# Batch 0 of an attention and two-MoE kernel: which engine masks its high parts and copies its second heads, on which line its value loads stand, and what the planner books for a conversion

## The chip, the cores and the metric

The kernel runs on one core of a Trainium2 chip. The metric is the device time of one execution in microseconds (us). Engines are PE (TensorE; its weight loads are PEld), DVE (VectorE), ACT (ScalarE), POOL (GpSimd) and SP (SyncE, which here only issues DMAs). Each engine works off its own queue in order and stands still at an instruction whose semaphore has not come.

## The reference

Three layers in a row, all in float32:

```python
# attention: B, H, S, D = 4, 8, 576, 64; rotate() is rotary position embedding
scores = (rotate(q) @ rotate(k).T) / sqrt(D)
attn   = softmax(scores)                      # max, exp, sum
x      = (attn @ v) -> [2304, 512]
# MoE 1: 512 -> 2048 -> 512, leaky relu with a slope alpha per column
h = x @ w_in;  g = max(h, 0) + alpha * min(h, 0);  x = g @ w_out
# soft MoE 2: 8 experts x 4 slots
logits = x @ phi;  d = softmax over tokens;  c = softmax over slots
slot_in = d.T @ x;  slot_out[e] = relu(slot_in[e] @ w1[e]) @ w2[e];  out = c @ slot_out
```

## The kernel before

**How the work is tiled.** Attention runs over 4 batches (b) of 4 pairs of heads (p). For a pair, `prep_qk` loads keys and queries with their half-swapped copies (tile `xn`, 128 partitions x 2 x 576), multiplies by the rotary tables and adds (lines 320 and 323; on DVE for the very first pair, on POOL for all others), and splits the sum into a high part (`hi`, line 326, which writes `xn[:, 1]`) and a low rest (`lo`, line 329, on DVE). DMAs on SP's queue stack the two parts into the tiles `ks` (line 346) and `qs` (line 343), so that one matmul sums both. `row_events` then makes the five row blocks of a pair (four of 128 rows for each of two heads, and a tail): scores on PE (line 385) into PSUM, a maximum on DVE (line 390), exp on ACT (line 395), a reciprocal on DVE (lines 402 and 403), the scaling on POOL (line 427), and then a transposition of the probabilities into the tile `ET`. Batches 1 to 3 transpose through DVE blocks and a round trip through DRAM. Batch 0 (`MOVED = 1`) transposes on PE (line 448) and copies PSUM to `ET` (`turned`, line 457). `pv_events` multiplies by the values (line 527) and writes `xt`, the input of MoE 1.

**Weights.** Meanwhile `prep_w` makes 16 pieces ready, eight of `w_in` and eight of `w_out`: a load of 1 MB (`wraw`, line 578, three buffers), three DVE instructions that convert 64-bit floats to 32-bit ones (lines 598, 600 and 602), and for `w_in` a bound on ACT (610), a scaling on POOL (613), and a rest on PE (267, 268). Odd pieces of `w_in` sit for a time in buffers of `xt` (`wx`), so the first `pv` of a full block waits for the last of them. Pieces of `w_out` are written to DRAM (`wo_dram`, line 623) from a single buffer (`wf`), and multiplied with `phi` (lines 647 to 659).

**MoE 1** runs over nine blocks of 256 tokens (line 684) as soon as all four pairs of a half batch are done, between the attention of later batches. The second MoE's weights are loaded at the end.

**What sets the order.** `Plan.order` simulates all operations at build time: each has an engine, a cost in ns and a due time, and a free engine takes the ready operation with the lowest due time. The order in which the operations start in the plan is the order in which each engine's instructions, and SP's DMAs, are issued on the chip. So a changed cost or a changed engine changes no duration on the chip by itself, but can change every queue's order from there on. DMAs are booked on one engine of the plan. `order_ops` keeps lines of operations that must stay in order: "load" for the loads of keys and queries, "v" for those of values.

Of the kernel before, what the change touches and what calls it, by code (L numbers as in the profile page):

```python
# [12 lines left out]
F32R = mybir.dt.float32r  # L13
I32 = mybir.dt.int32
AF = mybir.ActivationFunctionType
ALU = mybir.AluOpType
# [33 lines left out]
class Plan:  # L50
# [9 lines left out]
    def op(self, eng, cost, due, fn, deps=(), takes=(), uses=()):  # L60
        o = Op(eng, cost, due, fn, deps, takes, uses)
        for d in o.deps:
            d.after.append(o)
        for s in uses:
            s.left += 1
        self.ops.append(o)
        return o
# [95 lines left out]
def attn_moe_softmoe(ctx, tc, qx, kx, vx, w_in, w_out, alpha, phi, w1, w2, tab, msks, out):  # L163
    nc = tc.nc
# [47 lines left out]
    op = plan.op  # L212
# [67 lines left out]
    def prep_v(b, due):  # L280

        mv = vb[:, b]
        iv = viv[b] = mv[:, 8:10]
        bound = []
        for p in range(NP):
            e, sl = {}, Slot("vt")

            def load(p=p, e=e):
                e["t"] = att.tile([128, 9, D], F32, tag="vt", name="vt", bufs=5)
                nc.sync.dma_start(e["t"], vx[b, p])  # L290

            def bnd(p=p, e=e):
                junk = moe["p"].tile([128, 288], F32, tag="rl", name="junk", bufs=2)
                nc.scalar.activation(junk[:].bitcast(F16).rearrange("p (r d) -> p r d", d=D), e["t"], AF.Abs, accum_out=mv[:, 4 + p:5 + p])

            o = order_ops["v"] = op(DMA, 900, due - PRE + 2 * p, load, [order_ops["v"]], takes=[sl], uses=[sl])
            vt[b, p] = (e, sl, o)
            sj = Slot("rl")
            bound.append(op(ACT, 870, due, bnd, [o], takes=[sj], uses=[sl, sj]))
        top = op(DVE, 150, due, lambda: nc.vector.tensor_reduce(mv[:, 0:1], mv[:, 4:8], axis=AX.X, op=ALU.max), bound)  # L300
        red = top_all(due, mv[:, 0:1], mv[:, 1:2], top)
        viv_op[b] = chain(due, pow2_ops(mv[:, 2:3], mv[:, 1:2], iv[:, 0:1], iv[:, 1:2]), red)

    def prep_qk(b, p, due):

        r = {}
        s_st = {"q": Slot("Q"), "k": Slot("K")}
        ends = []
        first = b == 0 and p == 0
        eng, on, cost = (nc.vector, DVE, 650) if first else (nc.gpsimd, POOL, 1570)  # L310
        for i, (src, z) in enumerate(((kx, "k"), (qx, "q"))):
            sx, e = Slot("xn"), {}
            d = due - PRE + 3 * i if not first else -29 + 2 * i

            def load(src=src, e=e):
                e["x"] = att.tile([128, 2, S], F32, tag="xn", name="xn", bufs=3)
                nc.sync.dma_start(e["x"], src[b, p])

            def mul(w, z=z, e=e):
                eng.tensor_tensor(e["x"][:, w], e["x"][:, w], tabs[:, (0 if z == "q" else 2) + w], ALU.mult)  # L320

            def add(e=e):
                eng.tensor_tensor(e["x"][:, 0], e["x"][:, 0], e["x"][:, 1], ALU.add)  # L323

            def hi(e=e):
                nc.scalar.activation(e["x"][:, 1].bitcast(F32R), e["x"][:, 0], AF.Copy)

            def lo(e=e):
                nc.vector.tensor_tensor(e["x"][:, 0], e["x"][:, 0], e["x"][:, 1], ALU.subtract)

            def stack(w, z=z, e=e):
                if w is None:
                    if z == "q":

                        r[z] = att.tile([128, 2 * SP], F32, tag="Q", name="qs", bufs=2)
                        nc.vector.memset(r[z][:, S:S + 128], 0.0)
                    else:
                        r[z] = att.tile([128, 2, 2, S], F32, tag="K", name="ks", bufs=2)
                    return
                t, x = r[z], e["x"]  # L340
                for h in range(2):
                    if z == "q":
                        (nc.scalar if first else nc.sync).dma_start(t[64 * w:64 * w + 64, (S + 128) * h:(S + 128) * h + S], x[64 * h:64 * h + 64, 1 - w])
                    else:
                        for half in range(2):
                            nc.sync.dma_start(t[64 * half:64 * half + 64, w, h], x[64 * h:64 * h + 64, 1 - w])  # L346

            o = order_ops["load"] = op(DMA, 1700, d, load, [order_ops["load"]], takes=[sx], uses=[sx])
            o = op(on, cost, d, lambda mul=mul: mul(0), [o, tabs_op[z]], uses=[sx])
            o = op(on, cost, d, lambda mul=mul: mul(1), [o], uses=[sx, s_tabs])  # L350
            o = op(on, cost, d, add, [o], uses=[sx])
            o = op(ACT, 640, d + LEADS[0], hi, [o], uses=[sx])
            x = op(DVE, 970, d + LEADS[0], lo, [o], uses=[sx])
            n = 900 if z == "q" else 1800
            prev = order_ops.get(z)
            y = op(*((DVE, 120) if z == "q" else (None, 0)), d - 100, lambda stack=stack: stack(None), [prev], takes=[s_st[z]], uses=[s_st[z]])
            o = op(DMA, n, d - 100, lambda stack=stack: stack(0), [o, prev, y], uses=[sx, s_st[z]])
            o = op(DMA, n, d - 100, lambda stack=stack: stack(1), [x, o], uses=[sx, s_st[z]])
            order_ops[z] = o
            ends.append(o)  # L360
        qk[b, p] = (r, ends, [s_st["q"], s_st["k"]])

    def row_events(b, p, s, n, pair):
# [46 lines left out]
        evs = []  # L410
# [12 lines left out]
        for h in heads:  # L423
            def norm(h=h):
                if tail:
                    nc.gpsimd.tensor_scalar(c["e"][:, 1, 0:64], c["e"][:, 0, 512:S], c["mm"][:, 6:7], 1.0, ALU.mult, ALU.mult)
                nc.gpsimd.tensor_scalar(c["e"][:, h], c["e"][:, h], c["mm"][:, 6 + h:7 + h], 1.0, ALU.mult, ALU.mult)  # L427

            o2 = op(POOL, 1200 if tail else 820, n + h + LEADS[1], norm, [o], uses=[s_mm, s_e])
            norms.append(o2)  # L430
            if moved:
                def block(h=h):
                    if h == 0:
                        c["tb"] = att.tile([128, 16, 2, 32], F32, tag="tb", name="tb", bufs=2)
                    nc.vector.transpose(  # L435
                        out=c["tb"][:, :, h].rearrange("p (q m) j -> p q m j", q=4),
                        in_=c["e"][:, h, 64 * h:64 * h + 512].rearrange("p (m q j) -> p q m j", m=4, q=4))

                blocks.append(op(DVE, 760, n + h + LEADS[2], block, [o2] + blocks[-1:], takes=[] if h else [s_tb], uses=[s_e, s_tb]))
                continue  # L440
            s_pm = Slot("pm")

            def turn(h=h):
                if h == 0 and first:
                    open_ET()
                c["pt", h] = ps_m.tile([128, 4, 128], F32, tag="pm", name="pt")
                for i in range(4):
                    nc.tensor.transpose(c["pt", h][:, i], c["e"][:, h, 64 * h + 128 * i:64 * h + 128 * i + 128], idf)  # L448

            def turned(h=h):  # L450
                if tail:
                    dst, src = pair["ett"][:, 0:4], c["pt", h]
                else:
                    dst = pair["ET"][:, 0:2048].rearrange("p (s q m h j) -> p s h m q j", s=2, q=4, m=4, h=2)[:, s % 2, h]
                    src = c["pt", h][:].rearrange("p m (q j) -> p m q j", q=4)
                if h == 0 or b == 0:
                    nc.scalar.activation(dst, src, AF.Copy)
                else:
                    nc.vector.tensor_copy(dst, src)

            new = h == 0 and first
            o2 = op(PE, 430, n + h + LEADS[2] - ATT, turn, [o2, pair.get("turn")], takes=[s_pm, s_ET] if new else [s_pm], uses=[s_pm, s_e, s_ET])
            pair.setdefault("turn", o2)
            evs.append(op(*((DVE, 690) if h and b else (ACT, 600)), n + h + LEADS[2], turned, [o2] + evs[:1], uses=[s_pm, s_ET]))
        if moved:
            if s % 2 == 0:
                pair["s_sc"] = Slot("sc")
# [98 lines left out]
    def prep_w(j, which, due):  # L566
# [48 lines left out]
        even = w_ops.get((which, j - 1)) if j % 2 else None  # L615
        u = [s_raw, s_wx, s_w]
        o = run["raw"] = op(DMA, 2913, due + WD, load, [run["raw"]], takes=[s_raw], uses=[s_raw])
        o = op(DVE, 1000, due, lambda: conv(0), [o, even if which == 0 else None], takes=[s_wx], uses=u)
        o = op(DVE, 1400, due, lambda: conv(1), [o], uses=u)
        o = op(DVE, 1600, due, lambda: conv(2), [o], uses=u)  # L620
        if which:
            w_ops[1, j] = o
            wo_saved.append(op(DMA, 1500, due, lambda: nc.sync.dma_start(wo_dram[:, 2 * j:2 * j + 2, :], c["wo"]), [o], uses=[s_w]))
# [705 lines left out]
```

## Time and profile before

| | us |
|---|---|
| median of 3 runs | 732.61 (729.93 to 734.29) |
| profiled execution, its own time | 733.35 |
| its span, first to last instruction | 731.6 |
| PE busy | 619.4 (85% of the span) |
| DVE busy | 426.1 (58%) |
| ACT busy | 341.9 (47%) |
| POOL busy | 280.6 (38%) |

The span leaves 1.75 us of the execution's own time outside. Busy shares are averages over stages: up to about 210 us batch 0's attention and the weight pieces run together, from there to about 550 us attention and MoE 1 share PE, then MoE 1 is alone, and the last 60 us load and use the experts' weights.

### The profile page before, as it was taken

The page shows a single profiled execution, that of the slowest core. Times are in us where ns is not written, and L with a number is a line of the kernel's source. Part 1 is how long each engine was busy: PE and PEld are TensorE (multiplying, and loading weights), DVE is VectorE, ACT ScalarE, POOL GpSimd, SP SyncE. Part 2 cuts the span into 40 slices and gives each one's busy share as a digit, 9 for nine tenths or more (in the row PEclk, how much of TensorE's full clock was granted, in tenths as well). Part 3 has the DMA queues.
Part 4 walks back from the last instruction along what each step waited for, and adds up shares of the span by engine and source line. Part 5 has one row for each costly group of instructions (what it writes and reads, how often), then busy time and mean ns, then how long its engine had stood idle before and what let it go on. Part 6 is the DMA issues. An engine that isn't in the chain of part 4 may idle for free.

```text
span 731.6 us, 13978 instructions
## 1 busy us (share of the span) xinstructions
PE 619.4 (85%) x5168; PEld 460.3 (63%) x5168; DVE 426.1 (58%) x933; ACT 341.9 (47%) x840; POOL 280.6 (38%) x283
## 2 busy tenths in 40 slices
PE   0747479694999989989898999998999999997973
PEld 0543246584877767776676777786687787773442
DVE  5675854565677675769556777785662333334422
ACT  2444425573565555555554555565453343330111
POOL 0496972646253564538444574452221000000000
PEclk9958579897899999999999999999999999999998
DMA  9977646566368897998969997978744961146998
GB/s 299 327 218 203 193 153 207 164 175 229 98 225 216 256 240 227 302 267 220 270 203 292 269 275 221 237 207 245 201 118 116 407 254 59 53 164 260 409 397 300
DMA packets 82146, 167.84 MB, mean 229 GB/s; under 512 B 10656, under 2 KB 39840, under 8 KB 82080
## 3 DMA queue, kind: packets, MB, share of 16 engines
q1 hardware_dynamic: 81760, 166.37, 74.4%
q8 instruction: 41, 0.67, 0.4%
q10 hardware_dynamic: 320, 0.59, 0.4%
q14 instruction: 25, 0.20, 0.1%
HBM read 104.54 MB, written 34.08 MB: 189 GB/s over the span
## 4 chain that ended last, share of the span: by engine, by line
PE 53%; DMA 24%; DVE 6%; SPq 5%; POOL 5%; issue 3%; ACT 3%; ACTq 0%; POOLq 0%; DVEq 0%
PE ph L684 19%; PE pv L527 10%; DMA xw<-in_moe_w_dram 6%; DMA ET<-sc 6%; PE st L385 5%; PE pt L703 3%; DMA ks<-xn 3%; DMA qs<-xn 3%; DMA xn<-in_k_dram 2%; PE lg L714 2%; PE pu L808 2%; SPq L346 2%; POOL e L427 2%; PE pt L448 2%; PE wphp L656 2%
## 5 line engine op out<-in xcount | busy, mean ns | idle before, releaser
L684 PEld LDWEIGHTS <-w 128*128 128x128 f16 x1728 | 164.5, 98 | 32.1 <-issue 11.1
L684 PE MATMUL ph<-xt,w 128*128 128x256 f16 x1536 | 183.5, 273 | 0.0
L427 POOL TENSOR_SCALAR e<-e,mm 128x576 f32<-128x576 f32 x144 | 119.6, 841 | 142.4 <-DVE mm L403 86.2
L390 DVE TENSOR_REDUCE mm<-st 128x1 f32<-128x576 f32 x144 | 105.7, 743 | 36.7 <-PE st L385 31.4
L385 PE MATMUL st<-ks,qs 128*128 128x288 f32 x512 | 102.6, 330 | 26.6 <-DMA ks<-xn 19.3
L395 ACT ACTIVATE e<-st,mm 128x576 f32<-128x576 f32 x144 | 106.3, 739 | 35.4 <-DVE mm L390 31.8
L697 DVE SCALAR_TENSOR_TENSOR g<-rl,oma,ph 128x256 f32<-128x256 f32 x144 | 68.2, 474 | 77.4 <-ACT rl L692 76.5
L320 POOL TENSOR_TENSOR xn<-xn,tabs 128x576 f32<-128x576 f32 x60 | 89.4, 1503 | 62.0 <-DMA xn<-in_k_dram 29.6
L692 ACT ACTIVATE rl<-ph 128x256 f32<-128x256 f32 x144 | 55.0, 382 | 102.7 <-PE ph L684 101.8
L385 PEld LDWEIGHTS st<-ks,qs 128*128 128x128 f32 x512 | 77.9, 203 | 35.5 <-DMA ks<-xn 19.2
L527 PE MATMUL pv<-ET,vt 128*64 128x256 f32 x512 | 66.1, 402 | 18.0 <-DMA ET<-sc 14.5
L435 DVE STREAM_TRANSPOSE tb<-e 128x512 f32<-128x512 f32 x96 | 66.5, 698 | 20.5 <-DMA sc<-tb 13.2
L527 PEld LDWEIGHTS pv<-ET,vt 128*64 128x64 f32 x512 | 38.3, 141 | 38.5 <-issue 14.0
L708 ACT ACTIVATE gt<-pt 128x512 f32<-128x512 f32 x72 | 43.0, 597 | 18.1 <-PE pt L703 16.4
L448 PE MATMUL pt<-idf,e 128*128 128x128 f32 x192 | 33.3, 308 | 14.3 <-POOL e L427 14.3
L537 ACT ACTIVATE xt<-pv,vb 128x256 f16<-128x256 f32 x32 | 15.1, 473 | 64.8 <-PE pv L527 64.7
L703 PE MATMUL pt<-idf,g 128*128 128x128 f32 x288 | 43.7, 274 | 0.4 <-DVE g L697 0.4
L323 POOL TENSOR_TENSOR xn<-xn 128x576 f32<-128x576 f32 x30 | 43.5, 1453 | 0.7
L448 PEld LDWEIGHTS pt<-idf,e 128*128 128x128 f32 x192 | 25.3, 160 | 21.3 <-POOL e L427 16.5
L703 PEld LDWEIGHTS pt<-idf,g 128*128 128x128 f32 x288 | 33.7, 141 | 2.5 <-issue 0.8
L402 DVE TENSOR_SCALAR mm<-mm 128x2 f32<-128x2 f32 (+1 forms) x80 | 24.7, 309 | 15.7 <-ACT e L395 15.7
L540 DVE SCALAR_TENSOR_TENSOR xt<-pv,vb,xt 128x256 f16<-128x256 f32 x32 | 15.4, 480 | 26.3 <-ACT xt L537 26.0
(151 smaller groups left out, 819.9 us busy)
## 6 DMA issues: line engine op xcount, KB each, us to landing
sc<-tb SPq DMA_DIRECT2D x48, 512.0 KB, 6.1
ET<-sc SPq DMA_DIRECT2D x96, 256.0 KB, 5.6
xw<-in_moe_w_dram SPq DMA_DIRECT2D x42, 512.0 KB, 10.2
ks<-xn SPq DMA_DIRECT2D x128, 144.0 KB, 3.6
xn<-in_k_dram SPq DMA_DIRECT2D x16, 576.0 KB, 6.1
xn<-in_q_dram SPq DMA_DIRECT2D x16, 576.0 KB, 5.9
qs<-xn SPq DMA_DIRECT2D x60, 144.0 KB, 4.8
wraw<-in_moe_w_in_dram SPq DMA_DIRECT2D x8, 1024.0 KB, 8.3
```

The source lines that it names most:

```text
L320: eng.tensor_tensor(e["x"][:, w], e["x"][:, w], tabs[:, (0 if z == "q" else 2) + w], ALU.mult)
L385: nc.tensor.matmul(st[:, j, 0:288], r["q"][:, 768 * h + 128 * s:768 * h + 128 * s + 128].bitcast(F32R), r["k"][:, a, h, ks].bitcast(F32R), ...
L390: nc.vector.tensor_reduce(c["mm"][:, h:h + 1], c["st", h][:, :, 0:288], axis=AX.XY, op=ALU.max, negate=True)
L395: nc.scalar.activation(c["e"][:, h].rearrange("p (a n) -> p a n", a=2), c["st", h][:, :, 0:288], AF.Exp, bias=c["mm"][:, h:h + 1], accum_o ...
L427: nc.gpsimd.tensor_scalar(c["e"][:, h], c["e"][:, h], c["mm"][:, 6 + h:7 + h], 1.0, ALU.mult, ALU.mult)
L435: nc.vector.transpose(out=c["tb"][:, :, h].rearrange("p (q m) j -> p q m j", q=4), in_=c["e"][:, h, 64 * h:64 * h + 512].rearrange("p (m q ...
L448: nc.tensor.transpose(c["pt", h][:, i], c["e"][:, h, 64 * h + 128 * i:64 * h + 128 * i + 128], idf)
L527: nc.tensor.matmul(pv[r], v[k, 4 * h + i if i < 4 else 8], x, start=(i == 0), stop=(i == 4))
L684: nc.tensor.matmul(ph, wi[j][:, wp, kc, 128 * fo:128 * fo + 128], xt[:, xp, kc, :], start=(n == 0), stop=(n == 3 * KC - 1),)
L692: nc.scalar.activation(c["r"], c["ph"], AF.Relu, scale=-1.0)
L697: nc.vector.scalar_tensor_tensor(blk["g", j][:, fo, :], c["r"], oma[:, f:f + 1], c["ph"], ALU.mult, ALU.add)
L703: nc.tensor.transpose(c["pt"][:, t, i, :], blk["g", j][:, fo - 1 + i, 128 * t:128 * t + 128], idf)
```

## The change

Batch 0 only: the high part is made by DVE as a bit mask (the low 12 bits cleared) in place of ACT's rounding copy, and the copies of the second head (`h = 1`) from PSUM to `ET` go from ACT to DVE. The four value loads of batch 0 stand on the same line as the loads of keys and queries. The planner books 870, 1420 and 1250 ns for the three conversion steps, where it booked 1000, 1400 and 1600.

```diff
-            o = order_ops["v"] = op(DMA, 900, due - PRE + 2 * p, load, [order_ops["v"]], takes=[sl], uses=[sl])
+            z = "v" if b else "load"
+            o = order_ops[z] = op(DMA, 900, due - PRE + 2 * p, load, [order_ops[z]], takes=[sl], uses=[sl])
...
             def hi(e=e):
-                nc.scalar.activation(e["x"][:, 1].bitcast(F32R), e["x"][:, 0], AF.Copy)
+                if b:
+                    nc.scalar.activation(e["x"][:, 1].bitcast(F32R), e["x"][:, 0], AF.Copy)
+                else:
+                    nc.vector.tensor_scalar(e["x"][:, 1].bitcast(I32), e["x"][:, 0].bitcast(I32), -4096, None, ALU.bitwise_and)
...
-            o = op(ACT, 640, d + LEADS[0], hi, [o], uses=[sx])
+            o = op(*((ACT, 640) if b else (DVE, 870)), d + LEADS[0], hi, [o], uses=[sx])
...
-                if h == 0 or b == 0:
+                if h == 0:
                     nc.scalar.activation(dst, src, AF.Copy)
                 else:
                     nc.vector.tensor_copy(dst, src)
...
-            evs.append(op(*((DVE, 690) if h and b else (ACT, 600)), n + h + LEADS[2], turned, [o2] + evs[:1], uses=[s_pm, s_ET]))
+            evs.append(op(*((DVE, 690) if h else (ACT, 600)), n + h + LEADS[2], turned, [o2] + evs[:1], uses=[s_pm, s_ET]))
...
-        o = op(DVE, 1000, due, lambda: conv(0), [o, even if which == 0 else None], takes=[s_wx], uses=u)
-        o = op(DVE, 1400, due, lambda: conv(1), [o], uses=u)
-        o = op(DVE, 1600, due, lambda: conv(2), [o], uses=u)
+        o = op(DVE, 870, due, lambda: conv(0), [o, even if which == 0 else None], takes=[s_wx], uses=u)
+        o = op(DVE, 1420, due, lambda: conv(1), [o], uses=u)
+        o = op(DVE, 1250, due, lambda: conv(2), [o], uses=u)
```

## Rows read from the trace of the kernel before

**Rows 1.** Busy us (instructions) by stretch, then PE clock, DMA share, GB/s.

```profile
0.00:210.00 210.00, 141.26 (x860) 104.49 (x862) 130.60 (x241) 100.49 (x225) 113.46 (x105) 0.84 0.68 209
210.00:732.00 522.00, 478.17 (x4316) 355.85 (x4312) 295.53 (x692) 241.44 (x616) 167.13 (x179) 0.98 0.78 238
...
60.00:113.00 53.00, 32.57 (x123) 18.48 (x122) 36.02 (x54) 20.43 (x43) 38.26 (x32) 0.74 0.60 184
113.00:140.00 27.00, 26.14 (x209) 18.56 (x208) 10.99 (x27) 18.05 (x44) 8.68 (x11) 1.00 0.69 209
```

**Rows 2.** Chain that ended last, 0 to 210 us: first and last DVE, ACT, POOL pieces.

```profile
6.16 1.44 DVE xn L320 x2
...
8.41 0.69 ACT xn L326
...
31.29 0.61 POOL xn L320
...
190.63 0.60 ACT wt L651
...
202.14 0.17 DVE wph L659
...
208.65 0.21 POOL xn L320
```

**Rows 3.** Groups of instructions with their shapes, 0 to 210 us: busy us, mean ns.

```profile
L602 DVE SCALAR_TENSOR_TENSOR w<-wraw,w 128x1024 int32<-128x1024 int32 x12 | 18.8, 1567 | 0.0
...
L457 ACT ACTIVATE ET<-pt 128x512 f32<-128x512 f32 x32 | 18.3, 597 | 17.2 <-PE pt L448 16.7
...
L600 DVE SCALAR_TENSOR_TENSOR w<-wraw,w 128x1024 int32<-128x1024 int32 x12 | 17.1, 1429 | 0.1
...
L598 DVE TENSOR_SCALAR w<-wraw 128x1024 int32<-128x1024 int32 x12 | 9.1, 760 | 16.6 <-DMA wraw<-in_moe_w_in_dram 7.6 <-DMA wo_dram<-w 6.4 <-PE pt L448 2.1
...
L326 ACT ACTIVATE xn<-xn 128x576 fp32r<-128x576 f32 x13 | 8.8, 685 | 5.4 <-POOL xn L323 3.7 <-DVE xn L323 1.8
...
L402 DVE TENSOR_SCALAR mm<-mm 128x2 f32<-128x2 f32 x17 | 8.2, 479 | 7.9 <-ACT e L395 7.9
...
L600 DVE SCALAR_TENSOR_TENSOR wx<-wraw,wx 128x1024 int32<-128x1024 int32 x4 | 6.9, 1718 | 0.0
...
L602 DVE SCALAR_TENSOR_TENSOR wx<-wraw,wx 128x1024 int32<-128x1024 int32 x4 | 4.9, 1226 | 0.0
...
L598 DVE TENSOR_SCALAR wx<-wraw 128x1024 int32<-128x1024 int32 x4 | 2.7, 682 | 0.0
```

**Rows 4.** Single lines over the whole span: duration ns min/median/max.

```profile
L1220 DVE COPY ob<-pf x10: 680/691/693, 701.0 to 724.4; 128x512 f32<-128x512 f32 x10
...
L402 DVE TENSOR_SCALAR mm<-mm x80: 105/159/1381, 25.9 to 545.3; 128x2 f32<-128x2 f32 x64, 128x1 f32<-128x1 f32 x16
```

**Rows 5.** DVE, POOL and ACT in order of time between 74 and 88 us.

```profile
75.70 2.02 DVE L600 SCALAR_TENSOR_TENSOR wx<-wraw,wx 128x1024 int32<-128x1024 int32 x1
...
80.65 1.16 DVE L402 TENSOR_SCALAR mm<-mm 128x2 f32<-128x2 f32 x1 [0.31 <-ACT e L395]
...
80.38 2.76 POOL L320 TENSOR_TENSOR xn<-xn,tabs 128x576 f32<-128x576 f32 x2
...
74.22 0.68 ACT L326 ACTIVATE xn<-xn 128x576 fp32r<-128x576 f32 x1
...
87.61 0.68 ACT L326 ACTIVATE xn<-xn 128x576 fp32r<-128x576 f32 x1
```

**Rows 6.** SP's DMA issues in order of time, start us and issue time.

```profile
9.12 7.31 SPq L346 DMA_DIRECT2D ks<-xn  x8
...
18.30 3.04 SPq L290 DMA_DIRECT2D vt<-in_v_dram  x1
...
22.41 0.50 SPq L317 DMA_DIRECT2D xn<-in_k_dram  x1
```

**Rows 7.** DVE in order of time: the longest wait for a store.

```profile
171.57 0.75 DVE L598 TENSOR_SCALAR w<-wraw 128x1024 int32<-128x1024 int32 x1 [6.44 <-DMA wo_dram<-w]
```

## The prediction

> **What bounds the kernel now.** I read the table of stretches first. Before 210 us PE is busy for 141.3 of 210 us; after it for 478.2 of 522 [rows 1]. So PE has 68.7 us of holes early and only 43.8 late, and what the change can win or lose lies before 210 us, where all instructions it moves run. A us by which batch 0's attention ends earlier or later is carried to the end: MoE 1, which fills PE later, waits for all four pairs of a half batch, and the experts' weights wait for MoE 1's buffers. I count it one for one.
>
> Before 210 us no engine is full. DVE is busy for 130.6 us, POOL for 113.5, ACT for 100.5 [rows 1]. Of the two engines between which the change moves work, the receiver is the fuller one. The same order holds from 60 to 113 us, where the weight pieces are converted: DVE 36.0, ACT 20.4 of 53 us. It is turned round from 113 to 140 us, where ACT has 18.1 and DVE 11.0 of 27 us [rows 1].
>
> Next, the chain of what ended last. Between 0 and 210 us, of the 195 longest pieces, 32 are DVE's (22.0 us), 17 ACT's (10.2) and 18 POOL's (29.1); first and last of each are in [rows 2]. The reader is to see that one chain changes engine every us or two, so that no single operation sets this stretch. I therefore price moved work by a weight: an engine's time on the chain over its busy time. DVE 22.0/130.6 = 0.17, ACT 10.2/100.5 = 0.10, POOL 29.1/113.5 = 0.26. It says how often a us of such work has lain on the path; it is a choice, and the weakest part of the sum.
>
> **The high parts.** Four pairs with keys and queries make eight instructions. ACT loses 8 x 0.685 = 5.5 us [rows 3]. On DVE a mask of 128x576 does not occur before. Nearest is the first conversion step, also one source, a constant and 32-bit integers in SBUF: 128x1024 in 0.682 us where little disturbs it (the `wx` form, four times) [rows 3], by elements 0.38 us for 576. That is the lower bound. Above it comes time lost to POOL: the small line 402 takes 0.105 at best and 1.381 at worst [rows 4], an excess of up to 1.28 us, and the row at 80.65 us shows one that took 1.16 us while POOL's line 320 ran [rows 5]. So 0.38 to 1.66 us each. I take 0.38 plus the mean excess of line 402 before 210 us, 0.479 - 0.159 = 0.32 [rows 3, 4], that is 0.70: 5.6 us for eight, between 3.0 and 13.3.
>
> The handover also moves. Before, ACT's high part of the first keys starts at 8.41 us [rows 2] and the first stack is issued at 9.12 [rows 6]. POOL has no rotary work yet there, so the mask should take about 0.38 in place of 0.68: the first stack, and with it the first scores, come 0.3 us earlier. For the other six, DVE's mask stands in the queue that holds conversions of 1.2 to 2.4 us; the rest (`lo`) is DVE's anyway and follows directly.
>
> POOL pays in turn: six masks that meet its work hold it up by 0.38 us each at most, 2.3 us.
>
> **The copies.** Four pairs of four row blocks give 16 copies of a second head. ACT loses 16 x 0.597 = 9.6 us [rows 3]. DVE's copy of 128x512 from PSUM takes 0.691 at the median, 0.680 to 0.693 over ten [rows 4], so 16 x 0.69 = 11.0 us, with hardly a spread. The write into `ET` is strided and that row's is not; I take nothing for this, and 0.7 us each as the upper bound, a second pass of the same length (+11 us on DVE, at its weight 1.9).
>
> **The value loads.** No move: in the plan the batch's loads are due at -9 to -3, after the first queries' load (-27) and before the next keys' (0), so the joint line demands the order that SP already shows, values at 18.30 us and keys at 22.41 [rows 6]. Batch 1's first load only loses a predecessor that was long done. SP, ACT's bounds and the DMA engines see the same. If the order did change, the price is that of one blocked issue, 3.0 us [rows 6].
>
> **The planned durations.** No duration on the chip changes. The plan books 3.54 us for a piece in place of 4.00; the trace has (9.1 + 2.7)/16 + (17.1 + 6.9)/16 + (18.8 + 4.9)/16 = 0.74 + 1.50 + 1.48 = 3.72 us [rows 3]. So the plan was 0.28 too long and becomes 0.18 too short: as good as before, I book nothing. But with 16 x 0.46 = 7.4 us less and 8 x 0.87 + 16 x 0.69 = 18.0 more on the planned DVE, and 8 x 0.64 + 16 x 0.60 = 14.7 less on ACT, every queue's order after the first pair is drawn anew. That has no sign of its own. Its size is that of a stall that appears or goes: the longest of DVE's is 6.4 us, at 171.57, for a store of `wo_dram` [rows 7]. This widens the range more than any term.
>
> **The sum.** DVE +16.6 x 0.17 = +2.8. ACT -(5.5 + 9.6) x 0.10 = -1.5. POOL +2.3 x 0.26 = +0.6. Start -0.3. Together +1.6 us on the profiled execution's own 733.35, so 735.0, which is 0.3% above the median of 732.61. With DVE's masks at their bounds (3.0 and 13.3) it is +1.2 and +2.9; with strided copies also, +4.8. If all moved work lay on the path, it would be +24 us one way and -15 the other.
>
> **Rivals.**
>
> *DVE's queue becomes the bound while weights are converted (slower).* Between 60 and 113 us DVE is at 68% [rows 1], and three high parts fall there, ACT's first of them at 74.22 us and its last at 87.61. At the first, DVE is within a run of conversions (the next, at 75.70, takes 2.02 us) [rows 5]; a stack of queries waits behind it. On DVE it waits for one conversion, 1.2 to 2.0 us, and so do the two others: 3 x 1.5 = +4.5, and the scores' maxima behind them wait too. With the sum: about +6, so 741 (736 to 748). It decides once two of the three are late by more than 1.2 us. For it: DVE's load and its in-order queue. Against: a third xn buffer lets loads run ahead. The Trainium skill (SBUF — State Buffer, section "SBUF: two separate sides") says that a VectorE instruction in a two-port mode and a GpSimd instruction exclude each other for a whole instruction; by that rule each mask that meets POOL's work waits it out, and this rival gains. The trace agrees as far as the row at 80.65 us shows it.
>
> *ACT's relief opens batch 0 (faster).* Both heads' copies now run side by side: two on ACT take 2 x 0.597, a pair on two engines 0.69, so 0.5 us for each of the 12 row blocks after the first pair, -6 us if all were on the path, so 728. For it: ACT is ahead of DVE from 113 to 140 us. Against: ACT itself waited 16.7 us for PE in front of these copies [rows 3], so most came as fast as PE gave them, and PE is busy for 26.1 of the 27 us [rows 1].
>
> *The new order drops a stall (faster).* If the conversion at 171.57 no longer meets the late store, up to 6.4 us go [rows 7], of which DVE's followers use most: 728. As easily a new one appears, which I count in the first rival.
>
> *The change does nothing.* If the moved work is hidden altogether and the order stays, 733. The forecast's own range takes this in.
>
> **How the numbers follow.** What a measurement of this kernel can tell from no change is about 0.5%, 3.7 us. My forecast (a small net cost, or nothing, 731 to 739) has 0.42, of which 0.32 lies within 0.5%, 0.09 above and 0.01 below. DVE as the bound or a new stall: 0.27, slower. ACT's relief 0.14 and a dropped stall 0.14: faster. The last 0.03 is a larger change of either sign (0.02 faster, 0.01 same). Faster 0.31, same 0.33, slower 0.36. The time is that of the likeliest case, 735. Its own range is 731 to 739; the one for 8 in 10 takes in most of both signs' cases: 722 to 747.
>
> **What would show it.** In the profile after: the mask on DVE at about 0.7 us (0.4 undisturbed), eight of them; 16 DVE copies of 0.69; DVE's busy time before 210 us up by some 16 us and ACT's down by 15; value and key loads in the same order, the first stack 0.3 us earlier. Right means that MoE 1's first matmul comes within about 5 us of where it was, late rather than early. Wrong would be a wait of several us that has no counterpart before, above all DVE or SP standing still for a load or a store, or holes in PE before 210 us that shrink by more than 4 us.

## The result, and the profile after

The change made the kernel faster: 726.15 us median against 731.04 for the kernel before in the same session, ratio 0.9896 with a 95% interval of 0.987 to 0.9923 (19 runs each). The forecast was 735.0, with 0.31 for faster. The profiled execution has a span of 723.2 us against 731.6. Here and below the medians are of all executions, while a ratio leaves out those over 1.5% above the fastest of their kernel, so that it need not be the quotient of the medians.

By stretches of the changed kernel (PE, PEld, DVE, ACT, POOL busy us, then PE's granted clock, DMA share, GB/s):

```profile
60.00:113.00 53.00, 34.78 (x130) 19.82 (x129) 38.26 (x62) 18.80 (x40) 43.13 (x34) 0.68 0.52 153
113.00:140.00 27.00, 25.79 (x206) 17.98 (x206) 15.70 (x34) 14.97 (x36) 5.76 (x9) 1.00 0.81 254
140.00:160.00 20.00, 17.91 (x144) 15.57 (x144) 16.35 (x33) 13.15 (x33) 17.12 (x15) 1.00 0.60 164
160.00:180.00 20.00, 18.13 (x138) 15.04 (x135) 16.35 (x28) 11.33 (x29) 16.19 (x12) 0.83 0.61 225
...
0.00:210.00 210.00, 148.27 (x940) 110.17 (x941) 150.97 (x284) 94.85 (x220) 130.25 (x114) 0.85 0.69 217
210.00:723.00 513.00, 472.50 (x4231) 350.39 (x4229) 283.54 (x674) 234.01 (x596) 156.27 (x169) 0.97 0.78 238
```

Before 210 us PE's holes shrink from 68.7 us [rows 1] to 61.7, and MoE 1's first matmul starts at 189.9 us instead of 195.9. To see where, I followed PE's busy time summed from the start. The changed kernel leads by 0.7 us at 113 us, 0.4 at 140, 3.1 at 165, 10.5 at 180 and 7.0 at 210. The 10.5 holds matmuls that run at half pace (the last section has rows), which count as busy for longer. So most of this lead comes from one place, 165 to 180 us. Around it the kernel before has this:

```profile
160.00:180.00 20.00, 10.76 (x95) 8.82 (x91) 10.68 (x18) 8.73 (x21) 12.59 (x11) 0.83 0.72 225
```

PE is busy for 10.8 of 20 us before, and for 18.1 after. The view of PE in order of time shows what the hole of before is:

```profile
168.52 0.27 PE L491 MATMUL pc<-idf,e 128*128 128x128 f32 x1
177.15 1.09 PE L647 MATMUL wtp<-idf,w 128*128 128x128 f32 x4 [8.36 <-DVE w L602]
```

PE stands still for 8.4 us, for a piece of `w_out` that DVE converts late, because the piece's first step waited 6.44 us for a store [rows 7]. ACT and POOL stand behind transfers of their own at the same time (kernel before, in order of time):

```profile
174.72 0.68 ACT L294 ACTIVATE junk<-vt 128x576 f16<-128x576 f32 x1 [5.61 <-DMA vt<-in_v_dram]
```
```profile
170.38 5.54 POOL L320 TENSOR_TENSOR xn<-xn,tabs 128x576 f32<-128x576 f32 x3 [2.75 <-DMA xn<-in_k_dram]
175.89 2.37 POOL L323 TENSOR_TENSOR xn<-xn 128x576 f32<-128x576 f32 x1
179.21 1.47 POOL L427 TENSOR_SCALAR e<-e,mm 128x576 f32<-128x576 f32 x2 [0.95 <-DVE vb L300]
```

ACT waits for batch 1's fourth value load before it does the fourth pair's next exponential. POOL rotates batch 1's keys and queries, which came late, before it scales (L427) the fourth pair's exponentials. In the changed kernel the same work stands in another order (L321 and L324 are the rotation, L431 the scaling, L294 the value's bound):

```profile
165.79 2.77 POOL L321 TENSOR_TENSOR xn<-xn,tabs 128x576 f32<-128x576 f32 x2 [3.55 <-DMA xn<-in_k_dram]
168.53 2.87 POOL L431 TENSOR_SCALAR e<-e,mm 128x576 f32<-128x576 f32 x2
...
174.13 2.43 POOL L431 TENSOR_SCALAR e<-e,mm 128x576 f32<-128x576 f32 x2
```
```profile
174.73 0.68 ACT L294 ACTIVATE junk<-vt 128x576 f16<-128x576 f32 x1
```

Two scalings at a time stand between the rotary steps, and the value's bound finds its load landed. The rows of the new masks (eight) and copies (sixteen) on DVE, by single lines, give the duration in ns (min/median/max) and the first and last start:

```profile
L330 DVE TENSOR_SCALAR xn<-xn x8: 447/460/1652, 8.3 to 96.2; 128x576 int32<-128x576 int32 x8
```
```profile
L463 DVE COPY ET<-pt x16: 667/690/692, 31.7 to 184.9; 128x512 f32<-128x512 f32 x16
```

### The profile page after: what moved, and what is told of

Same layout as the page of the kernel before. It is cut to its first block, busy times and chain, and to the rows that moved or that the text cites. A ratio compares the mean times of both kernels' runs of the same rounds, so it can differ in the third digit from the quotient of the medians.

```text
span 723.2 us, 13983 instructions
## 1 busy us (share of the span) xinstructions
PE 620.8 (86%) x5168; PEld 460.6 (64%) x5168; DVE 434.5 (60%) x957; ACT 328.9 (45%) x816; POOL 286.5 (40%) x283
## 4 chain that ended last, share of the span: by engine, by line
PE 52%; DMA 22%; POOL 8%; SPq 6%; DVE 6%; issue 3%; ACT 2%; POOLq 0%; DVEq 0%; ACTq 0%
PE ph L688 19%; PE pv L531 10%; DMA ET<-sc 7%; DMA xw<-in_moe_w_dram 6%; PE st L389 5%; DMA ks<-xn 4%; SPq L350 4%; DMA xn<-in_k_dram 3%; PE pt L707 3%; POOL e L431 3%; DMA qs<-xn 2%; PE pu L812 2%; PE lg L718 2%; POOL xn L321 2%; PE pt L452 2%
## 5 line engine op out<-in xcount | busy, mean ns | idle before, releaser
L431 POOL TENSOR_SCALAR e<-e,mm 128x576 f32<-128x576 f32 x144 | 121.3, 852 | 153.8 <-DVE mm L407 58.2
L389 PE MATMUL st<-ks,qs 128*128 128x288 f32 x512 | 99.8, 327 | 23.4 <-DMA qs<-xn 18.8
L321 POOL TENSOR_TENSOR xn<-xn,tabs 128x576 f32<-128x576 f32 x60 | 90.0, 1517 | 51.9 <-DMA xn<-in_q_dram 36.5
L324 POOL TENSOR_TENSOR xn<-xn 128x576 f32<-128x576 f32 x30 | 44.4, 1479 | 0.8
L452 PE MATMUL pt<-idf,e 128*128 128x128 f32 x192 | 31.5, 297 | 8.3 <-POOL e L431 7.7
L452 PEld LDWEIGHTS pt<-idf,e 128*128 128x128 f32 x192 | 23.6, 153 | 16.2 <-POOL e L431 10.7
L333 DVE TENSOR_TENSOR xn<-xn 128x576 f32<-128x576 f32 x32 | 27.4, 855 | 6.1 <-ACT xn L328 4.7
```

Of the source, the lines that this page charges most:

```text
L389: nc.tensor.matmul(st[:, j, 0:288], r["q"][:, 768 * h + 128 * s:768 * h + 128 * s + 128].bitcast(F32R), r["k"][:, a, h, ks].bitcast(F32R), ...
```

## The experiments

The expectations use these names. **Theory 1**: the order that the planner draws anew makes the gain; its forms with a letter name the stall in that order (the store, batch 1's fourth value bound, and, as 1d, three queues together). **Theory 2**: the moved work itself makes it. Each run was timed against the kernel before on its own chip; a time after a stroke is that of the kernel before there.

**Order and engines apart (e1, e2).** What the planner books and what an engine executes are separate lines, so each can be changed alone. e1 is the changed kernel with the execution of before; e2 is the kernel before with the execution of after.

```diff
 # e1, against the changed kernel
-                if b:
-                    nc.scalar.activation(e["x"][:, 1].bitcast(F32R), e["x"][:, 0], AF.Copy)
-                else:
-                    nc.vector.tensor_scalar(e["x"][:, 1].bitcast(I32), ...)
+                nc.scalar.activation(e["x"][:, 1].bitcast(F32R), e["x"][:, 0], AF.Copy)
...
-                if h == 0:
+                if h == 0 or b == 0:
 # e2: the reverse of these two, against the kernel before
```

> The plan is that of the change to the last operation, so every queue has the changed kernel's order, but batch 0's high parts and second copies are executed by ACT, as before. Theory 1 (the gain comes from the new order of the queues, not from the engines): the ratio to the kernel before stays at 0.985 to 0.995, as for the whole change (0.990), and the last product with the values of batch 0 comes at 174 to 181 us. Theory 2 (ACT's relief is the gain): the ratio goes back to 0.996 or more.

> The counterpart: the plan is that of the kernel before, so SP's, POOL's and PE's queues are as before, but DVE executes batch 0's masks and second copies at the places where ACT had them. Theory 1 (order): ratio 0.997 to 1.010, since DVE gets some 16 us of work in a stretch where it is the fuller engine, and the wait of 6.4 us for the store of the output weights stays within a us or two. Theory 2 (ACT's relief): ratio 0.985 to 0.993.

e1: 728.26 / 736.34, ratio 0.9869 (0.9826 to 0.9913). e2: 736.44 / 736.34, ratio 0.9998 (0.9965 to 1.0031). The whole gain is there without any work on another engine, and the moved work in the old order costs and brings nothing within 2.6 us. In e2's profile the old stall is there too: DVE waits 6.6 us for the store, and PE stands still for 6.8 us. Theory 2 falls.

**Which stall (e3 to e7).** e3 and e4 put each `wo_dram` store into SP's queue right behind its conversion, in the kernel before and in the changed one; no other queue changes. e5 moves batch 1's fourth value bound on ACT, with the maximum and scale that follow, behind the last product of batch 0. e6 and e7 do both.

```diff
-    for o in plan.order():
+    order = plan.order()
+    for o in wo_saved:
+        order.remove(o)
+        order.insert(order.index(o.deps[0]) + 1, o)
+    for o in order:
         o.fn()
```
```diff
+    at = order.index(last_pv[0, 3, 1])
+    behind = [o for o in order[:at] if o in late[1]]
+    order = [o for o in order[:at + 1] if o not in behind] + behind + order[at + 1:]
```

> The kernel before with one edit: each store of a converted piece of the output weights stands in SP's queue right behind its conversion, ahead of the loads of queries and keys that stood before it; the other four queues are unchanged. Theory 1a (the stall at 165 to 171.6 us, where DVE waits for that store, is what the new order dropped): that wait shrinks from 6.4 to below 1 us, the last product with the values of batch 0 comes 4 to 8 us earlier than 187.4, ratio 0.988 to 0.995. Rival 1b (another part of the order, for example the earlier row blocks of the fourth pair): the wait goes, but the ratio stays at 0.997 to 1.003.

> The same edit in the changed kernel, whose waits for these stores are 5.4 us in two pieces. Theory 1a: these were mostly beside other work, so the ratio to the kernel before stays within 0.003 of the change's 0.990, or falls by up to 0.004 more. Rival 1b: no difference to the changed kernel either; if it gains as much as the kernel before gains by this edit, the two orders differ in something else than the stall.

> The kernel before with one edit: the bound of batch 1's fourth value tile (ACT) and what follows from it (a maximum on DVE and PE, the scale) stand in their queues behind the last product with the values of batch 0, where they stood ahead of the fourth pair's row blocks. SP and POOL are unchanged. Theory 1a (DVE's wait for the store alone made the hole at 165 to 177 us): ACT's wait of 5.6 us goes, the store's stays, ratio 0.998 to 1.003. Theory 1c (two waits lie over each other there, DVE's for the store and ACT's for batch 1's values, and either alone keeps most of the hole): the same here, but e6 gains more than e3. If the bound alone was the cause: 0.987 to 0.993 here.

> The kernel before with both edits, stores first and bound late; engines, costs and the rest of the order are those of before. Theory 1c: both waits are gone, the last product with the values of batch 0 comes 8 to 10 us earlier than 187.4, and the ratio is 0.985 to 0.992, all of what the whole change gains, without any of its parts. Theory 1a: the same as e3, about 0.995. If something else in the new order makes the gain: 0.996 or more.

> The changed kernel with both edits. If the new order had already dropped both waits (theory 1c), little is left to gain: 0.985 to 0.992 to the kernel before, not more than 0.004 below the change itself. If the hole in the kernel before and the gain of the change are two things, the edits add to the change: 0.978 to 0.984.

| | this / before, us | ratio | interval |
|---|---|---|---|
| e3 | 732.69 / 736.34 | 0.9914 | 0.9867 to 0.9961 |
| e4 | 728.71 / 736.34 | 0.9864 | 0.9802 to 0.9925 |
| e5 | 740.16 / 736.03 | 1.0111 | 1.0049 to 1.0173 |
| e6 | 733.96 / 736.03 | 0.9978 | 0.9929 to 1.0028 |
| e7 | 732.21 / 736.03 | 0.9991 | 0.9955 to 1.0028 |

The store in its place takes DVE's wait away and wins something (the plain medians of e3 give 0.9950), but PE's lead at 180 us is 0.3 us and not 10.5 (roughly: e3's profile has a span of 736.0 us against a median of 732.69). PE now waits for DVE, which waits for ACT's bound of the late values:

```profile
180.68 0.80 PE L228 MATMUL top<-idf,vb 128*128 128x128 f32 x2 [6.47 <-DVE vb L300]
```

Moving the bound so far back is a loss of 1% in both kernels (e5; e7 against e4). That batch 1's own values wait for it is likely, but not shown. In e5 PE's hole stays, 8.3 us for the store. With both moved the hole stays as well, and PE's view of e6 names the third queue:

```profile
179.66 1.12 PE L450 MATMUL pt<-idf,e 128*128 128x128 f32 x4 [6.79 <-POOL e L429]
```

L429 is the scaling, behind POOL's rotary work. So no single stall makes the hole, and the forms of theory 1 with one stall fall. On the clock e3 alone would not show this, since its interval takes in the change's ratio; e6 and e10 below hold the same move of the store and win 0.2%, not told from none.

e4 shows something else: in the changed kernel the same move opens a hole where the change had closed it. POOL waits there for a load of queries, and PE for POOL:

```profile
172.12 1.12 PE L452 MATMUL pt<-idf,e 128*128 128x128 f32 x4 [5.58 <-POOL e L431]
```

Yet e4 wins as much as the change. So a hole of this length in this place need not cost the gain.

**Ten ns (e8).** The kernel before, with the conversion's first step booked at 1010 ns; every instruction stays on its engine.

```diff
-        o = op(DVE, 1000, due, lambda: conv(0), ...
+        o = op(DVE, 1010, due, lambda: conv(0), ...
```

> The kernel before with one planned duration changed by 10 ns: the first conversion step is booked at 1010 ns in place of 1000. No instruction, engine or transfer differs, only the order that the plan makes of them. If the order is as good as drawn by lot (theory 1), the time differs from before by up to 1% with either sign, 0.990 to 1.010, with no link to any cost. If orders near each other cost the same: 0.998 to 1.002.

724.74 / 736.03, ratio 0.9899 (0.9861 to 0.9937). A cost that is 1% off, and to the other side than the change's 870, gives as much as the whole change. PE's lead is 0.2 us at 165 us and 5.2 at 180.

**The three queues (e9 to e12).** In the order of before, three small moves: the stores as in e3; the two multiplications of batch 1's key behind the fourth pair's scaling; the value's bound behind the exponentials of one further block only. e9 makes all three, e10, e11 and e12 leave out POOL's, ACT's and SP's.

```diff
+    for o in rot[1, 2, "k"][1::-1]:           # POOL: not in e10
+        order.remove(o)
+        order.insert(order.index(all_norms[0, 3, 1, 1]) + 1, o)
+    at = order.index(exp_op[0, 3, 2])         # ACT: not in e11
+    behind = [o for o in order[:at] if o in late[1]]
+    order = [o for o in order[:at + 1] if o not in behind] + behind + order[at + 1:]
```

> The kernel before with three places in its order changed and nothing else: each wo_dram store right behind its conversion; the two multiplications of batch 1's key of pair 2 (POOL) moved behind the scaling of the fourth pair's second block; batch 1's fourth value bound (ACT) with its small followers moved behind the exponentials of the next block. Theory 1d (the gain of the whole change is TensorE's hole at 165 to 180 us, and the hole is three in-order queues that each stand behind a transfer issued late): TensorE's busy time up to 180 us rises by 6 to 10 us over the kernel before, and the time falls by 5 to 8 us (728 to 731 where the kernel before takes 736), as with the change. Rival 2 (the hole is only one of many, the rest of the order makes the gain): the hole closes by under 3 us, or what is won is given back by 300 us, and the time is within 3 us of the kernel before.

> As the three places, but POOL's order as before: POOL still has the key's rotation ahead of the fourth pair's scaling. Theory 1d: POOL's queue alone keeps the hole open; TensorE's lead at 180 us is under 3 us and the time within 4 us of the kernel before (the store alone gave 0.991 to 0.995). Rival 2: no difference to the three places.

> As the three places, but ACT's order as before: ACT still waits for the value load at the fourth pair's second exponential (5.6 us before). Theory 1d: the lead at 180 us is half of that of the three places, or less. Rival 2: no difference to the three places.

> As the three places, but SP's order as before: DVE still waits 6.4 us for the wo_dram store ahead of the fourth pair's reciprocal. Theory 1d: the lead at 180 us is under 3 us. Rival 2: no difference to the three places.

What PE waits for between 165 and 180 us (us in total, times, longest), in e9:

```profile
PE pt L453 <- POOL e L431: 1.7, 1, 1.7
PE top L228 <- DVE vb L301: 1.4, 1, 1.4
PE wphp L661 <- ACT wt L656: 0.7, 1, 0.7
PE wtp L652 <- ACT ec L500: 0.4, 1, 0.4
```

and the one long wait of e10, of e11 and of e12:

```profile
178.16 1.12 PE L453 MATMUL pt<-idf,e 128*128 128x128 f32 x4 [6.68 <-POOL e L431]
```
```profile
174.73 0.80 PE L228 MATMUL top<-idf,vb 128*128 128x128 f32 x2 [6.66 <-DVE vb L301]
```
```profile
172.73 1.08 PE L652 MATMUL wtp<-idf,w 128*128 128x128 f32 x4 [6.21 <-DVE w L607]
```

Whichever queue keeps its old order, PE stands still for 6.2 to 6.7 us; in e11 it waits for DVE, which waits for ACT, whose row shows the value load:

```profile
173.71 0.68 ACT L294 ACTIVATE junk<-vt 128x576 f16<-128x576 f32 x1 [6.34 <-DMA vt<-in_v_dram]
```

With all three moved the longest wait is 1.7 us and PE's lead at 180 us is 6.5 us; with two it is 1.2, 1.5 and 2.2. The times: e9 729.82 / 734.55, ratio 0.9950 (0.9911 to 0.9989); e10 0.9985 (0.9947 to 1.0023); e11 0.9957 (0.9919 to 0.9994); e12 0.9999 (0.9947 to 1.0052). So theory 1d is right about the hole, and e9 wins 4.7 us in the medians, somewhat under the 5 to 8 us expected. On the clock the three and the pairs are not cleanly apart (e11 equals e9 within the intervals), and the whole change wins about twice as much as e9.

**More draws (e13 to e18).** Is the order before an unlucky one, and does one part of the change draw the better order? e13 to e15 are its parts alone, booked and executed as in the change; e16 books 990 ns in e8's place. Theories A, B and C are told in the expectations.

```diff
 # e13
-        o = op(DVE, 1000 ... 1400 ... 1600
+        o = op(DVE, 870 ... 1420 ... 1250
 # e14: booked
-            o = op(ACT, 640, d + LEADS[0], hi, [o], uses=[sx])
+            o = op(*((ACT, 640) if b else (DVE, 870)), d + LEADS[0], hi, [o], uses=[sx])
 # e15: booked; executed where h == 0, in place of h == 0 or b == 0
-            evs.append(op(*((DVE, 690) if h and b else (ACT, 600)), ...
+            evs.append(op(*((DVE, 690) if h else (ACT, 600)), ...
 # e16
-        o = op(DVE, 1000, due, lambda: conv(0), ...
+        o = op(DVE, 990, due, lambda: conv(0), ...
```

> The conversions' three planned durations alone (870, 1420, 1250 ns for 1000, 1400, 1600); every instruction is as before, only the order is drawn anew. Theory A (the order before was an unlucky draw, and most others are faster): 5 to 10 us faster, TensorE's lead at 180 us 5 to 10 us. Theory B (orders scatter to both sides): no telling, within 8 us on either side, and the lead at 180 us goes with the sign of the time. Theory C (these durations are what the planner lacked): at least as fast as the whole change, 724 to 728 where the kernel before takes 735.

> Batch 0's high parts masked by DVE, booked and executed there, nothing else. The engines by themselves are worth nothing (e2), so the time is that of the order drawn. Theory A: 5 to 10 us faster. Theory B: within 8 us on either side. Theory C: not faster than the kernel before by more than 3 us, since the durations are the old ones.

> Batch 0's second heads' copies on DVE, booked and executed there, nothing else. Theory A: 5 to 10 us faster. Theory B: within 8 us on either side. Theory C: not faster than the kernel before by more than 3 us.

> The conversion's first step booked at 990 ns instead of 1000, nothing else (10 ns more made it 9 to 11 us faster). Theory A: 5 to 10 us faster again. Theory B: within 8 us on either side. Theory C: as the kernel before, within 3 us.

The copies alone are the fastest kernel of all, and raised one more question, answered by e17 (e15's order, ACT copies) and e18 (the old order, DVE copies):

> The order of the copies-alone kernel, but ACT executes batch 0's second heads' copies as in the kernel before. If the order makes the gain (theories A and B): 1.5 to 2.5% faster than the kernel before, 715 to 722. If the copies' engine makes it: within 0.5% of the kernel before. Half of each: about 1%.

> The order of the kernel before, but DVE executes batch 0's second heads' copies; the high parts stay on ACT. If the order makes the gain: within 0.5% of the kernel before, as masks and copies together were (e2). If the copies' engine gains and the masks lose: 1 to 2% faster.

The last column is PE's busy time in 165 to 180 us of the profiled execution; the kernel before has 5.8, the change 13.1.

| | this / before, us | ratio | interval | PE, us |
|---|---|---|---|---|
| e13 durations | 731.46 / 733.03 | 0.9981 | 0.9941 to 1.0021 | 12.5 |
| e14 masks | 723.22 / 733.03 | 0.9886 | 0.9851 to 0.9921 | 10.5 |
| e15 copies | 716.34 / 733.03 | 0.9788 | 0.9747 to 0.983 | 13.1 |
| e16 990 ns | 734.72 / 733.03 | 1.0021 | 0.9985 to 1.0056 | 6.5 |
| e17 e15's order, ACT | 718.41 / 734.16 | 0.9779 | 0.9726 to 0.9832 | 12.3 |
| e18 old order, DVE | 733.15 / 734.16 | 0.9981 | 0.9953 to 1.001 | 6.1 |

e17 and e18 repeat e1 and e2: the order makes the gain, the engine nothing that can be measured. e15's 16.7 us are more than any of the theories allowed. Theory C falls: the new durations alone give no gain that can be told from none, and two kernels with the old ones win 1.1% and 2.1%. Of the six orders that I drew by a booked number (after, e8, e13 to e16), four are 1 to 2% faster and two equal to before within the measurement, none slower. That leans to theory A, the old order was an unlucky one, but e13 and e16 miss its 5 to 10 us, and six draws don't settle it. All of them but e16 lose the hole at 165 to 180 us.

The fastest has the hole closed and no row of PE at half pace after it. Its stretch from 140 to 210 us has a granted clock of 1.00; the kernel before had 0.85 there. First e15, then the kernel before:

```profile
140.00:210.00 70.00, 62.00 (x529) 51.96 (x528) 60.24 (x115) 41.49 (x104) 49.56 (x41) 1.00 0.59 183
```
```profile
140.00:210.00 70.00, 55.33 (x429) 47.44 (x430) 45.55 (x85) 35.59 (x84) 34.10 (x30) 0.85 0.57 173
```

e15 starts the last of the nine products that sum MoE 1's blocks into the slots of MoE 2 (line 808) 19 us before the kernel before (642 against 661 us), but the first of them only 7 us earlier (263 against 270). The other 12 us come after 270 us, most of them between the second and third block (333 to 409 us before, 324 to 389 in e15). What shortens that stretch is open.

## Why the prediction was wrong

**The step that failed** is "the planned durations". It said rightly that every queue's order is drawn anew, that the size is that of a stall, and that the longest of DVE's is the 6.4 us at 171.57. Then it booked nothing, because the order "has no sign of its own", and put the likeliest time on the engines' terms. The runs show the opposite shares: the engines' terms are nothing that can be measured (e2, e18), and the order is all (e1 0.9869 and the change 0.9896; e17 0.9779 and e15 0.9788). The sign could have been weighed. PE's hole of 8.4 us stood in the old trace, with three queues behind late transfers at once; few orders repeat that, so an order drawn anew was likelier to lose the hole than to make one as large. This is said after the fact: five of the six draws lose it and none of the five has as long a wait of PE between its first scores and 210 us, but e8, e15 and e16 have one of 6.8, 7.4 and 6.7 us between 70 and 113 us, where the kernel before has 4.2 at most. The prediction gave "the new order drops a stall" 0.14 and set it against new stalls as equal. Its own sign of being wrong came: PE's holes before 210 us shrank by 7.0 us, where it named 4.

**One for one.** The prediction counted what is won before 210 us as carried to the end. That did not hold from order to order. e7 starts MoE 1's first matmul at 189.4 us, 6.5 us before the kernel before, and wins nothing that can be told from none; e4 starts it at 192.7 us and wins 1.4%.

**Its sum.** DVE +2.8, ACT -1.5, POOL +0.6 and the start -0.3 make +1.6 us; e2, which is this sum without the order and the load line, measured -2.6 to +2.3. So the sum is not contradicted, and it answered the smaller question. Up to 140 us the changed kernel's blocks start their products with the values about 3 us later (119, 126, 134 us against 117, 123, 130), as "late rather than early" had it; but e1, with the old engines in the new order, is as late (120, 127, 134), so this is the order again and not the sum. At the seventh block the changed kernel was 10 us ahead. The busy times forecast for the stretch before 210 us, DVE up by 16 and ACT down by 15, came as 20.4 up and 5.6 down. They do not isolate the moved work: in e1, which moves none, DVE is up by 8.2 and ACT by 4.3.

**The masks.** Predicted 0.38 undisturbed and 0.70 with POOL in the way, measured 0.46 at the median, and two of eight at 1.65, just under the upper bound of 1.66: about 6 x 0.46 + 2 x 1.65 = 6.1 us for all, where 5.6 were forecast. The long ones, at 39.19 and 82.00 us, meet POOL's rotation:

```profile
39.19 1.65 DVE L330 TENSOR_SCALAR xn<-xn 128x576 int32<-128x576 int32 x1 [1.29 <-POOL xn L324]
...
81.94 2.98 POOL L321 TENSOR_TENSOR xn<-xn,tabs 128x576 f32<-128x576 f32 x2
...
82.00 1.65 DVE L330 TENSOR_SCALAR xn<-xn 128x576 int32<-128x576 int32 x1 [1.56 <-POOL xn L324]
```

The mask at 82.00 ends 0.2 us after the first of the two POOL instructions (1.49 each), the one at 39.19 ends 0.3 us after a POOL instruction of 1.40 that started at 39.12. That agrees with the rule of the Trainium skill that the prediction named (SBUF — State Buffer, section "SBUF: two separate sides"). In one more such meeting POOL seems to have paid: the mask at 74.37 took 0.46 us, and the POOL instruction that started at 74.32 (L261) 0.66, where most of that line take 0.37.

**The copies** took 0.69, as the row of the other copy had it [rows 4]; the strided write cost nothing. **The start**: the first stack was issued at 8.78 us, 0.34 earlier [rows 6], where 0.3 was forecast. It bought nothing that lasted, since the eight issues then took 9.63 us instead of 7.31:

```profile
8.78 9.63 SPq L350 DMA_DIRECT2D ks<-xn  x8
...
19.57 1.90 SPq L290 DMA_DIRECT2D vt<-in_v_dram  x1
...
22.54 0.50 SPq L318 DMA_DIRECT2D xn<-in_k_dram  x1
```

**The value loads** did not move, as forecast: values at 19.57 us, keys at 22.54. Built with that line alone, the kernel has the same instructions in the same order on every engine as before, so this part of the change can do nothing by itself.

**The rivals.** *DVE's queue becomes the bound* met its condition, but not its cause or its price. The three high parts start at 74.37, 82.00 and 96.18 us, against 74.22, 80.51 and 87.61 before, so two are late by more than 1.2 us. At 74.37 and 82.00 us DVE stood idle before the mask, for POOL, and was not within a conversion. The third stood behind conversions, 8.6 us late; but e1, where ACT makes it in the same order, has it at 95.22, so the lateness is the order's. e2, with masks on DVE in the old order, has 75.21, 82.51 and 91.18 and no measured loss. *ACT's relief opens batch 0* was priced at -6 us; e18, which is this rival for the copies alone, has 0.9981 (0.9953 to 1.001), -3.5 to +0.7 us. *The new order drops a stall* was the right kind, and its 728 is near the 726.15 measured. ACT's relief had the same 728, so the number alone proves nothing; e1 and e18 tell the two apart. But its mechanism was too small. The store alone (e3) leaves the hole; three waits stand side by side there, each good for 6.2 to 6.7 us alone, and in the old order only all three moves together close it.

**What stays open.** That the order makes the gain is shown; which part of the order is not. The hole's closing accounts for 6.5 to 10 us of lead at 180 us in e9 and in the changed kernel, but the lead is not the gain: e13 has 9.7 us at 180 and wins nothing measurable, e14 only 1.9 at 210 us and wins 1.1%, and e4 wins 1.4% with a hole of 5.6 us. Later stretches draw their own orders, and no run separates them.

## What to carry to other kernels

Where a planner writes out the order, a change of its costs is first of all a new draw of the order: execute the old engines in the new order and the new engines in the old one, before a gain is put down to the work that was moved. Price such a draw by the worst hole of the bounding engine in the old trace, and ask how likely another order is to repeat it; a hole at which several in-order queues stand behind late transfers at once is sooner lost than made again. Give it a chance and not a sum: here five of six draws lost the hole, and four of these five were faster. Since 10 ns in one cost moved this kernel by 1%, several draws are cheap to time, and the fastest here (the copies alone, 716.34 us) beats both kernels.

## What I had not expected of the hardware

Transfers land late enough to make in-order queues collide. The plan books 1.5 us for the store, 0.9 for a value load and 1.7 for a key load, and adds 1.0 until the stored buffer is free and 2.4 until a load can be used: 2.5, 3.3 and 4.1 us. The kernel before issues these three on SP at 164.25, 166.12 and 163.87 us, and the instructions that wait for them start at 171.57, 174.72 and 170.38: 7.3, 8.6 and 6.5 us later. Over the whole kernel the medians from issue to landing are 3.1, 4.0 and 6.1 us in the profile's list of transfers. So the key load is about as late as usual, and the store and the value load are unusually late here.

PE's rows after this hole run at about half pace, the lower of its two clock levels. Four transposes of a weight piece (L647) take 0.60 us at 164.60 in the kernel before, 1.09 at 177.15 behind the 8.4 us hole, and 1.06 at 182.16; at 189.88 it is 0.66 again. So this hole costs more than its length. But closing it does not by itself bring the full clock. In the changed kernel four transposes take 1.12 us behind a wait of 1.9 us, and the granted clock of 165 to 180 us is 0.77, as in the kernel before (0.78); in e15 four transposes behind a wait of 1.8 us take 0.66, and the clock is 1.00 from 140 to 210 us. First the kernel before, then the changed one, then e15:

```profile
164.60 0.60 PE L647 MATMUL wtp<-idf,w 128*128 128x128 f32 x4
```
```profile
169.78 1.12 PE L452 MATMUL pt<-idf,e 128*128 128x128 f32 x4 [1.87 <-POOL e L431]
```
```profile
151.81 0.66 PE L448 MATMUL pt<-idf,e 128*128 128x128 f32 x4 [1.80 <-POOL e L427]
```
